# A gated linear recurrence and a two-layer MLP on one core: the order of all steps is found anew

## The chip, the cores and the metric

The kernel runs on one core of a Trainium2 chip. The metric is the device time of one execution in microseconds (us), as the median of several runs. Times of single instructions, positions and waits come from one profiled execution of the kernel.

Engines: PE is TensorE (matmul; PEld its weight loads), DVE is VectorE, ACT is ScalarE, POOL is GpSimd, SP is SyncE, which here issues every DMA.

## The reference

For each of 4 batches and 8 heads a complex-valued state is carried over 768 tokens; its result, 3072 tokens by 384, goes through an MLP with a leaky activation.

```python
mag = np.sqrt(a_re * a_re + a_im * a_im)
scale = np.minimum(mag, 0.999) / (mag + 1e-06)
a_re_n, a_im_n = (a_re * scale, a_im * scale)
for t in range(S):
    new_re = ar * S_re - ai * S_im
    new_im = ar * S_im + ai * S_re
    kv = np.einsum('bhd,bhe->bhde', k[:, :, t], v[:, :, t])
    S_re, S_im = (new_re + kv, new_im)
    y[:, :, t] = np.einsum('bhd,bhde->bhe', q[:, :, t], S_re)
x = attn_out.transpose(0, 2, 1, 3).reshape(B * S, H * D)
h = x @ w_in
g = np.maximum(h, 0.0) + alpha * np.minimum(h, 0.0)
return (g @ w_out).astype(np.float32)
```

Head dimension 48, `w_in` 384 x 2048, `w_out` 2048 x 384, all in float32 (the weights arrive as 64-bit words and are turned into float32 on the chip).

## The kernel before

The work is written as 41 generators, called tasks. Each `yield` ends a step; a step issues one instruction, or a few, on one engine (a PE step holds a burst of matmuls). Nothing is scheduled by a framework: a string, `ORDER` (lines 30 to 74), names one task per letter, and the plan advances that task by one step. So the string sets the order in which every engine and SP's queue are handed their instructions. Each engine works through what it is handed in that order, and waits where an input or a buffer is not ready.

```python
def run(self, order):
    for c in order:
        next(self.tasks[self.LETTERS.index(c)], None)
...
with tc.manual_schedule():
    for i, g in enumerate(GATES):
        plan.add(gates(i, *g))
...
    for u in range(NU):
        plan.add(unit(u))
    plan.add(loads_x())
    plan.add(all_mlp())
    plan.run(ORDER)
```

The tasks and their letters:

- `A` to `I`, `gates` (from line 224): the normalized gates and their running products, for batch 0 in three parts (1, 2 and 3 chunks of 128 tokens: A, B, C), then two parts of 3 chunks for each further batch. L251 loads the gates; L254 to L282 are ACT steps, L260 to L302 DVE steps; L319, L339 and L341 are the many products of the tree (on DVE for batch 0, the small ones on POOL for the others); L324 stores the decays, L427 and L430 make the phases, L422 and L432 store them. Two buffers `gate` are shared by all parts.
- `J`, `loads`: q and k of a unit (`KQ`, L580, L582), its phases (`PP`, L591, one buffer) and its decays (`T`, L598, two buffers). `K`, `half_rows`: copies of v in another row order (L561). `L`, `loads_v`: v (`V`, L607 to L612; `VL`, L630, L633).
- `M`, `pieces`: 16 pieces of the raw weights (L492, 768 KB each). `N` and `O`, `weights`: their conversion, with three ACT steps (L508, L510, L512), one POOL step (L516) and two DVE steps (L518, L520) for each.
- `P` to `Z` and `a` to `m`, `unit`: the 24 units, one chunk of 128 tokens of one batch each. DVE turns q and k by the phases (L665, L667) and runs the levels of a tree of decays (L721), PE makes the products within a level (L682), ACT copies operands and results (L744, L760, L703), DVE masks (L706). PE then transposes k (L789, copied by ACT in L791 and L792), makes the new state (L801; DVE L830, L833) and sums the output (L821, L845). ACT copies it (L859) into the unit's T, from where L864 stores it. T is free for the unit after the next one only then.
- `n`, `loads_x`: the stored outputs as the MLP's input (L877). `o`, `all_mlp`: for 14 groups of one or two units and 16 feature blocks each, PE's three matmuls (L893), ACT's negative part (L900), DVE's sum (L902), PE's output matmul (L912), ACT's copy (L922) and the store (L925). L893 writes one of two PSUM buffers; L902 frees it, so feature block k+2 waits for L902 of block k.

The first MLP work needs unit 0 complete and stored, and the first weights converted. The last needs unit 23.

## Time and profile before

| | us |
|---|---|
| median of 3 runs | 854.92 |
| the runs | 854.92, 858.98, 851.49 |
| span of the profiled execution (first to last instruction) | 851.8 |
| busy PE / DVE / ACT / POOL | 697.3 / 653.9 / 439.5 / 206.6 |

The page gives no other time of the profiled execution than its span, which lies 3.1 below the median and 0.3 above the fastest run. Busy time is the time in which an engine had at least one instruction under way; a share of the span hides stages with different limits, so the times by stretch of the span are read beside it. A group's row names the line, engine and operation, what it writes and reads, the shape and count, then total busy time, the mean of one in ns, and the idle time of the engine just before. A row of waits names the instruction that waited, what ended the wait, the total, the number of times and the longest.

### The profile page before, as it was taken

Reading aid. Unit: us, or ns where it says so; the run is one execution under the profiler, and the core shown is the slowest. Engines: PE = TensorE matmul, PEld = TensorE weight load, DVE = VectorE, ACT = ScalarE, POOL = GpSimd, SP = SyncE. Lnnn points to the kernel's source line nnn. Section 1 sums busy time; section 2 is a strip of 40 time slices with the busy share of each in tenths; the row PEclk is TensorE's granted clock in tenths of the full one; section 3 lists DMA queues with packets and bytes.
Section 4 is the critical chain, followed back from the end, with each engine's and each line's share of the span. In section 5 each row is a group of like instructions: output and inputs, shape, how many; then the busy total and the mean of one; then the engine's idle time right before and its main releaser. Section 6 shows DMA issues by size and latency. Waiting matters only on the chain.

```text
span 851.8 us, 26881 instructions
## 1 busy us (share of the span) xinstructions
PE 697.3 (82%) x11488; PEld 530.0 (62%) x11488; DVE 653.9 (77%) x1020; ACT 439.5 (52%) x937; POOL 206.6 (24%) x293
## 2 busy tenths in 40 slices
PE   0001414776998899899999999999999999999998
PEld 0001313565776677677777777777777777777776
DVE  5999999997997899599989986987776756633212
ACT  6767758766346754575476436554444334322221
POOL 6131232466403810270046044000052000000000
PEclk9999656798999999999999999999999999999999
DMA  8697977856779576877875887687554486412010
GB/s 238 140 286 173 245 187 232 221 133 134 179 192 197 120 164 171 185 159 168 240 152 130 219 157 183 146 189 177 130 119 99 142 157 124 89 44 65 11 39 9
DMA packets 194559, 130.92 MB, mean 154 GB/s; under 512 B 74504, under 2 KB 186248, under 8 KB 194440
## 3 DMA queue, kind: packets, MB, share of 16 engines
q1 hardware_dynamic: 194440, 129.20, 64.0%
q8 instruction: 90, 1.47, 0.8%
q14 instruction: 29, 0.24, 0.1%
HBM read 100.82 MB, written 35.71 MB: 160 GB/s over the span
## 4 chain that ended last, share of the span: by engine, by line
PE 58%; DVE 25%; DMA 7%; issue 3%; ACT 3%; SPq 3%; POOL 1%; DVEq 0%; ACTq 0%; POOLq 0%
PE ps_o L912 23%; PE ps_h L893 22%; DVE KQ L721 5%; PE ps_lv L682 4%; DVE gate L339 4%; DMA T<-decs 3%; PE ps_y L821 3%; DVE gate L427 2%; DVE gate L341 2%; PE ps_y L845 2%; PE ps_kv L801 2%; SPq L630 1%; DVE g_sb L902 1%; PE ps_kt L789 1%; DVE gate L430 1%
## 5 line engine op out<-in xcount | busy, mean ns | idle before, releaser
L912 PE MATMUL ps_o<-w_out_sb,g_sb 128*128 128x384 f32 x768 | 295.8, 498 | 12.8 <-DVE g_sb L902 10.0
L893 PE MATMUL ps_h<-xT,w_in_sb 128*128 128x256 f32 (+1 forms) x1344 | 299.5, 355 | 0.0
L893 PEld LDWEIGHTS ps_h<-xT,w_in_sb 128*128 128x128 f32 x1344 | 233.7, 192 | 71.1 <-issue 1.8
L902 DVE SCALAR_TENSOR_TENSOR g_sb<-g_sb,al,ps_h 128x256 f32<-128x256 f32 (+1 forms) x224 | 97.3, 436 | 131.6 <-ACT g_sb L900 131.2
L900 ACT ACTIVATE g_sb<-ps_h 128x256 f32<-128x256 f32 (+1 forms) x224 | 79.0, 354 | 201.5 <-PE ps_h L893 200.7
L912 PEld LDWEIGHTS ps_o<-w_out_sb,g_sb 128*128 128x128 f32 x768 | 137.1, 191 | 63.6 <-DVE g_sb L902 12.9
L721 DVE TENSOR_TENSOR KQ<-KQ,T 96x1024 f32<-96x1024 f32 x120 | 147.3, 1231 | 31.5 <-PE ps_lv L682 25.1
L682 PE MATMUL ps_lv<-WQ 96*32 96x32 f32 x2304 | 34.7, 204 | 79.3 <-DVE WQ L665 51.9
L682 PEld LDWEIGHTS ps_lv<-WQ 96*32 96x32 f32 x2304 | 26.8, 116 | 97.0 <-DVE WQ L665 51.9
L339 POOL TENSOR_TENSOR gate<-gate 128x72 f32<-128x72 f32 x42 | 23.9, 569 | 147.6 <-ACT gate L369 144.7
L744 ACT COPY WQ<-KQ 96x1024 f32<-96x1024 f32 x48 | 50.0, 1042 | 14.9 <-DVE KQ L721 14.8
L516 POOL TENSOR_SCALAR top<-top 128x768 f32<-128x768 f32 x16 | 39.2, 2454 | 70.1 <-ACT top L508 70.1
L760 ACT COPY W<-KQ 96x512 f32<-96x512 f32 x48 | 30.8, 642 | 43.7 <-DVE KQ L721 37.3
L339 DVE TENSOR_TENSOR gate<-gate 128x576 f32<-128x576 f32 (+5 forms) x84 | 49.9, 594 | 1.7
L859 ACT COPY T<-ps_y 48x256 f32<-48x256 f32 x96 | 30.8, 366 | 38.9 <-PE ps_y L845 38.3
L821 PE MATMUL ps_y<-A,VL 64*48 64x64 f32 x2304 | 43.3, 229 | 7.0 <-issue 5.6
L821 PEld LDWEIGHTS ps_y<-A,VL 64*48 64x48 f32 x2304 | 41.3, 129 | 7.9 <-issue 6.4
L789 PE MATMUL ps_kt<-ident,KQ 96*128 96x96 f32 x192 | 26.4, 263 | 22.3 <-DVE KQ L721 12.2
L427 DVE TENSOR_TENSOR gate<-gate 128x1152 f32<-128x1152 f32 (+2 forms) x36 | 44.2, 1250 | 0.1
L703 ACT ACTIVATE A<-ps_lv,columns 128x64 f32<-128x64 f32 x144 | 37.3, 336 | 13.0 <-PE ps_lv L682 12.8
L789 PEld LDWEIGHTS ps_kt<-ident,KQ 96*128 96x128 f32 x192 | 22.3, 150 | 30.9 <-ACT T L792 10.9
L801 PEld LDWEIGHTS ps_kv<-V,T 64*64 64x64 f32 x1408 | 28.0, 148 | 15.4 <-ACT T L792 8.7
(106 smaller groups left out, 927.2 us busy)
## 6 DMA issues: line engine op xcount, KB each, us to landing
T<-decs SPq DMA_DIRECT2D x48, 384.0 KB
PP<-phs SPq DMA_DIRECT2D x48, 193.5 KB
KQ<-in_q_dram SPq DMA_DIRECT2D x48, 192.0 KB
decs<-gate SPq DMA_DIRECT2D x7, 1152.0 KB
phs<-gate SPq DMA_DIRECT2D x14, 576.0 KB
KQ<-in_k_dram SPq DMA_DIRECT2D x40, 192.0 KB
vsc<-in_v_dram SPq DMA_DIRECT2D x48, 144.0 KB
VL<-vsc SPq DMA_DIRECT2D x24, 288.0 KB
```

The source lines that it names most:

```text
L339: on(4 * k).tensor_tensor(out=m, in0=w[:, 1::-1].unsqueeze(2).to_broadcast([P, 2, 2, k]), in1=pairs_of(u), op=ALU.mult)
L427: TT(out=m[:, a], in0=U5[:, 1 + a], in1=turned(off3, o)[:, a].unsqueeze(1).unsqueeze(3).to_broadcast([P, L // 2, nb, 2]), op=ALU.mult)
L682: nc.tensor.matmul(t[64 * i + j:64 * i + j + HC // 2, p], lhsT=keys(n, g), rhs=queries(n, g), start=True, stop=True)
L721: nc.vector.tensor_tensor(out=x, in0=x if x0 is None else x0, in1=m, op=ALU.mult)
L744: nc.scalar.copy(z.rearrange("p i n t -> p i (n t)").rearrange("p i (m h) -> p m i h", h=h), bass.AP(tensor=KQ.tensor, offset=KQ.offset + ...
L789: nc.tensor.transpose(t[:, p], KQ[:, 1, 4 * i + p], ident[:D2, :D2])
L801: nc.tensor.matmul(kv[s][j:j + HC, n], lhsT=T[rows, n, j:j + HC], rhs=V[rows, n // 2, (n % 2) * D:(n % 2 + 1) * D], start=True, stop=True)
L821: nc.tensor.matmul(o, lhsT=Vp[h][64 * i:64 * i + 64, s, e_ * D:(e_ + 1) * D], rhs=a, start=False, stop=False)
L893: nc.tensor.matmul(p, lhsT=w_in_sb[:, f // 2, kk, f % 2 * P:(f % 2 + 1) * P], rhs=x_of[m][:, kk], start=(kk == 0), stop=(kk == NK - 1))
L900: nc.scalar.activation(gt, p, AF.Relu, scale=-1.0)
L902: nc.vector.scalar_tensor_tensor(out=gt, in0=gt, scalar=al_1[:, f:f + 1], in1=p, op0=ALU.mult, op1=ALU.add)
L912: nc.tensor.matmul(sums[0], lhsT=gt[:, c * P:(c + 1) * P], rhs=w_out_sb[:, f], start=(f == 0), stop=(f == NF - 1))
```

## The change

Only the string changes. The tasks, their steps, shapes, engines and buffers are the same; each task's own steps keep their order, and only the interleaving of tasks differs. The first lines and the last ones of both strings (44 lines each), and those with the first MLP steps:

```diff
 ORDER = (
-    "AAAAAAAAAAAAAAAAAAAAABAAAAJMJJMABBBMMBANJMMAOAAAAAAAAAAAAAAAAAALLLNBLAAAAAAAAAAALNAAAAAAAKKKKKKKLLLA"
-    "OALLAMNNAAAAAAOAAAAAAAAABLBNAAAAAAALAANBBNOOBNBBBLBMBBBJJOJNOBBBBBNBBJNNNBBNBBBBOBBBBBBBBBBBBBBBNOPB"
-    "POBPPPPCCCBOKBBBBBBBBBBBBBPPOBBPKBCBBBMPCBPKKBCBJKKOPOPBBBBBBOMBKPNPMBBKNJBCKBBBBPPMBKKNKKBBNBPBBBBP"
...
-    "CCCCQRMLLNDCJQCNRNRLLCQCCLLLRMCQCQDQRJJOCOCKQODCCCCRDNQQQQCCQQQQQQJODMQLNNDQODDODoQEKoooooooDOoRooND"
...
-    "oooooooooooooooooooooooooooooooooooooooooooooooooooooooooooooooooooooooooooooooooooooooooooooooooooo"
+    "AAAAAAAAAAMMMMMMAAAAAAANAAAJJAJJAAAAAAAAAAAAAAAAAANNNNBAAAAOAOOANKONNNAKANABAAAAAAAAAAOAANABAAAAANA"
+    "AAAAAAABBMOAAAMANAAKKKKKKKKKKKKKBOBMBAAABALAAAABABBBBBBBABOOOBCCOBBBBBBBJJJJBBOBOBBBBOBOOBCBBOBBBCCJ"
+    "BNNNBNBBCBBBBCCPBNBMMOBPBBBBBBCBBLBLLPLLLLLNNNNNBKMBBBPBOOOOMLPBMBNKBCBBBPPPNPKKKKBKKBKBKBKBPBPBPOBC"
...
+    "LQQQnQJJooQQDQQCCCJKCCCCCCQKCRCCCCOOOOCQLCKQCQQQCRCoCooooQCoRooCDoLDooKLLLDLCCCCCCooJooooooLRRRRRLCC"
...
+    "nooooooooooooooooooooooooooooooooooooooooooooooooooooooooooooooooooooooooooooooooooooooooooooooooooo"
     "oooooooooooooooo")
```

The weight pieces (M) and their conversion (N, O) stand earlier, between the steps of the first gate part; the loads of gate part B stand later; unit 0 (P) is spread over a longer stretch, unit 1 (Q) over a shorter one; the first MLP steps (o) stand earlier in the string. From there on to the end the same letters come in other places with the same overall course.

## The prediction

> **What bounds the kernel now.** I read the page's busy table and groups first, then the busy times by stretch, then the waits of VectorE (DVE) and TensorE (PE), then the chain that ended last and SyncE's queue (SP). The page:

> ```profile
> PE 697.3 (82%) x11488; PEld 530.0 (62%) x11488; DVE 653.9 (77%) x1020; ACT 439.5 (52%) x937; POOL 206.6 (24%) x293
> ...
> L912 PE MATMUL ps_o<-w_out_sb,g_sb 128*128 128x384 f32 x768 | 295.8, 498 | 12.8 <-DVE g_sb L902 10.0
> L893 PE MATMUL ps_h<-xT,w_in_sb 128*128 128x256 f32 (+1 forms) x1344 | 299.5, 355 | 0.0
> ```

> No engine is full over the whole span, so the stretches matter (columns: span from:to, its length, busy PE, PE weight loads, DVE, ACT, POOL, granted PE clock, DMA share, GB/s):

> ```profile
> 0.00:100.00 100.00, 14.03 (x460) 11.90 (x460) 87.44 (x191) 70.47 (x105) 29.61 (x41) 0.97 0.86 221
> 100.00:150.00 50.00, 13.49 (x385) 11.59 (x386) 49.14 (x85) 36.38 (x57) 15.02 (x7) 0.55 0.75 203
> 150.00:200.00 50.00, 38.37 (x690) 29.57 (x690) 47.14 (x71) 35.89 (x71) 30.43 (x33) 0.90 0.74 174
> 200.00:250.00 50.00, 43.70 (x870) 34.66 (x868) 43.31 (x66) 21.19 (x53) 15.99 (x16) 0.93 0.71 176
> 250.00:300.00 50.00, 44.62 (x882) 34.64 (x878) 42.48 (x59) 33.30 (x73) 27.14 (x35) 0.97 0.74 147
> 300.00:350.00 50.00, 46.18 (x848) 34.65 (x847) 43.06 (x63) 20.00 (x51) 7.72 (x23) 0.97 0.77 184
> 350.00:600.00 250.00, 249.18 (x4059) 186.47 (x4058) 216.03 (x290) 141.20 (x307) 64.53 (x105) 1.00 0.75 171
> 600.00:852.00 252.00, 247.77 (x3311) 186.54 (x3309) 125.33 (x202) 81.09 (x224) 16.15 (x35) 1.00 0.38 86
> ```

> There are three stages. To 200 us DVE is full and PE mostly idle. From 200 to 350 both are some 85 to 92% busy, held up by each other. From 350 PE has no idle left (4 us in 250, of which the waits show 0.9 in one stretch). So the end is fixed at about 350 us: the time is when PE becomes full, plus the PE work left. PE idles 150 us before that and almost nothing after. An order can gain only before 350, and can lose anywhere.

> The waits of DVE between 150 and 350 us, then those of PE from 350 on (total, times, longest):

> ```profile
> DVE g_sb L902 <- ACT g_sb L900: 6.9, 6, 2.6
> DVE KQ L721 <- DMA T<-decs: 6.0, 3, 2.5
> DVE KQ L721 <- PE ps_lv L682: 3.4, 1, 3.4
> DVE KQ L721 <- ACT WQ L744: 3.0, 2, 2.6
> DVE St L833 <- PE ps_kv L801: 2.8, 1, 2.8
> ```
> ```profile
> PE ps_y L845 <- DVE St L833: 0.5, 1, 0.5
> PE ps_y L821 <- issue: 0.4, 1, 0.4
> ```

> The chain that ended last has the loads of T (the decays of a unit) in the middle stage (start, length):

> ```profile
> 219.39 7.44 DMA T<-decs
> ...
> 255.98 7.68 DMA T<-decs
> ```

> **A way to count.** Each engine keeps the order it is handed. I give every instruction the time it adds to its engine's busy time in the trace (PE: the mean of its form after 400 us, at full clock) and sum these in either order. The sum ahead of an instruction is its position: DVE ends at 653, PE at 669. The lag is its time in the trace less its position. PE's lag is 160 at position 62, 172 at 126, 177.7 at 176, and then 179 to 180 to the end: 669 + 179.5 + some 3 for the last store is the span of 851.8. So the forecast is a forecast of PE's final lag.

> DVE's L902 of feature block k frees the PSUM buffer that PE's L893 of block k+2 needs. So PE's lag is at least (DVE position after L902 of k) - (PE position of L893 of k+2) + DVE's lag there. Before, this difference and DVE's lag are 138.9 and 31.2 at k=48 (PE lag 172.1), 137.0 and 38.1 at k=62 (177.7), 128.9 and 49.5 at k=88 (179.8): they leave 1.4 to 2.6 for ACT's L900 and PE's start. The bound is tight, and DVE's work ahead of the features, plus what DVE waits, is what PE's start is made of.

> **The change, part by part.** All 1009 DVE, 935 ACT, 265 POOL, 755 SP and 5888 PE steps of the planned tasks are the same with the same shapes; only their places differ.

> *Work ahead of the features.* The differences, before -> after, are: k=8 126.2 -> 130.0; k=24 137.3 -> 134.3; k=40 136.8 -> 134.2; k=48 138.9 -> 130.4; k=56 137.4 -> 130.7; k=62 137.0 -> 133.3; k=64 133.8 -> 132.1; k=72 134.3 -> 126.8; k=88 128.9 -> 125.2; k=112 121.0 -> 117.4. From k=16 on the new order puts 2 to 8 us less DVE work ahead of the same PE work. The largest is 140.3 (k=50) before and 136.2 (k=42) after, and the new one comes early, while DVE's lag is still small.

> *Start.* Six weight steps of DVE instead of two (L518 0.55, L520 0.96 us each) stand inside gate task A's chain, and on SP the weight pieces are issued from 2.9 us instead of 8.2, with B's gate loads (L251) behind the store L324 (issued at 14.9). The first piece (768 KB) then has 9 us until ACT's L508 wants it at 12.2; at the 238 GB/s of the page's first slice it takes 3.2. B's first ACT step moves from ACT position 8.3 to 17.4, so its load, issued at about 15.4, is in time. DVE's lag at the end of A stays 11.6. I cost the start at 0; without that cover it is 2 us.

> *Unit 0 goes back, unit 1 forward.* Unit 0's last L721 ends at DVE position 80.1 instead of 67.3, unit 1's at 108.2 instead of 115.7, and the first L902 at 118.0 instead of 133.6. On SP, unit 0's stores (L864, second at 101.3 before) are issued at about 111, and 21 issues stand between them and unit 2's T load, against 3 before; everything behind L864 waits with it. Before, the same kinds of issue took:

> ```profile
> 111.58 3.39 SPq L492 DMA_DIRECT2D g_sb<-in_w_out_dram  x1
> 115.07 0.41 SPq L492 DMA_DIRECT2D g_sb<-in_w_in_dram  x1
> ...
> 116.21 3.22 SPq L607 DMA_DIRECT2D V<-in_v_dram  x1
> 119.47 2.13 SPq L609 DMA_DIRECT2D V<-in_v_dram  x1
> ...
> 122.39 3.30 SPq L630 DMA_DIRECT2D VL<-in_v_dram  x4
> ```

> At the fast rows (0.4 to 0.8 each) they take some 12 us, with slow ones such as these 21. T is issued at 123 to 132 and lands 6.0 to 7.7 later, at 129 to 140. Unit 2's first L721 is due at DVE position 118.1 plus a lag of 13.5, at 131.6. The wait is 0 to 8; I take 3.5, and the features wait for the same queue (their x load is the issue before T).

> *Later T loads.* T has two buffers, so unit u's load follows unit u-2's stores. From L833 of u-2 to L721 of u took 15 to 18 us where DVE waited (units 5, 6). DVE's own work between them goes from 14.5 to 21.1 for unit 5, 12.3 to 17.2 for unit 6, 17.1 to 22.4 for unit 9: most of the 6.0 us of waits goes. Unit 4 goes the other way, from 25.3 to 13.7: up to 4 us late; with one issue left between its store and load, where there were four, I take 1. The gain from the others: 4.

> *Local loops.* Where DVE hands to PE or ACT and needs the answer, I took the work there less DVE's own work in between. Before, this is positive by 4.4 us at unit 9 (L833 to PE's L845, L682 and back to L721; DVE waited 3.4 there) and by up to 1.4 on ACT around DVE positions 240 to 246 and 318. In the new order the largest are 1.9 and 0.2. Gain 3 on DVE's lag near position 315. For POOL the loops have 0.6 us to spare or more: 0.

> *After 350 us.* Loops through DVE shorter than 25 us are at most 0.1 us before and -0.4 after beyond PE position 170: nothing added.

> **The sum.** PE's lag after = difference + DVE's lag at that DVE position + 2. With the lag of before: k=42 136.2 + 28 + 2 = 166; k=64 132.1 + 38 + 2 = 172; k=88 125.2 + 49 + 2 = 176. Without the 4 and 3 above and with the 3.5 and 1 added, DVE's lag is 2.5 lower at the last two: 169.5 and 173.5. The row at k=88 keeps waits of DVE for a full PE (L902), which need not come back; the row at k=64 may lack new ones. I take the middle, 172: 7.5 under 179.5. The span is 851.8 - 7.5 = 844.3. The median of the runs, 854.92, is 3.1 above the profiled span: **847.4, say 847**.

> [...] PE's first features come 16 us of DVE work earlier but then stand in a sparse stretch. In this trace the clock is 0.50 from 100 to 140 us, where PE is busy 1 to 2 us in 10, and 1.00 from 150 to 160. [...] By the trace's rows PE idles over 80% of that stretch, so this adds nothing.

> **The rivals.** (1) *PE fills at once.* If DVE's waits past position 243 vanish, the largest difference decides: 136.2 + 24 to 28 + 2 = 162 to 166, a gain of 13.5 to 17.5: 840. For it: no loop is left over 2 us. Against it: DVE's lag grew from 17 at position 175 to 39 at 315. (2) *SP's queue becomes the wait.* If unit 2's T lands at 140 (8 us), unit 4's comes 4 late and the order behind them shifts by 3 more, DVE's lag is 15 higher where I took 4.5: 847 + 10.5 = 858, slower than before. It decides once these waits pass 12 us together; its far end is one wait as long as SP's longest, 20.2 us (behind L925), on top of my 4.5: 867. For it: issues of 3 us under load, SP waits of 77 us behind L864 and 104 behind L925. Against it: the vsc copies (L561), 5.8 us for two in that stretch before, are moved out of it. (3) *It does not do what it says:* DVE's waits for PE and T stay as they were, the lag at k=88 decides with the new 3.5: 179.5, no change: 855.

> **How the numbers follow.** Forecast 0.43 (842 to 852), rival 1 0.20 (835 to 842), rival 2 0.30 (852 to 868), rival 3 0.07 (852 to 858). A measurement here tells about 1% from no change: 846.4 to 863.5. Faster: rival 1 and under half of the forecast's case, 0.39. Slower: half of rival 2, 0.15. Within 1%: 0.46. The range, 837 to 864, leaves out the low end of rival 1 (0.06) and the high end of rival 2 (0.14).

> **What would show it.** PE's idle before it is full should fall from 150 to about 142 us, and from 250 to 350 us from 9 to 4; DVE's waits for T between 150 and 350 us from 6 to 3 or less; the first L902 should start near 132 to 136 instead of 147. Wrong would be: a wait of more than 8 us at unit 2's L721; PE idle of several us after 350; or DVE's lag over 40 at position 300.

## The result and the profile after

| | before | changed |
|---|---|---|
| median of 4 runs, us | 855.44 | 886.55 |
| lowest to highest | 851.49 to 858.98 | 875.09 to 891.86 |
| span of the profiled execution | 851.8 | 873.4 |

The changed kernel is slower: ratio 1.0286, 95% interval 1.0238 to 1.0334. Two of its four runs were disturbed and are left out of the ratio and of the medians further below; the other two took 875.09 (the profiled one) and 883.24 us. The forecast was 847, in a range of 837 to 864.

The page of the changed kernel: the busy table, then groups (busy, mean ns | idle before, and what ended it):

```profile
PE 704.4 (81%) x11488; PEld 535.5 (61%) x11488; DVE 654.3 (75%) x1020; ACT 441.9 (51%) x937; POOL 188.9 (22%) x293
...
L893 PE MATMUL ps_h<-xT,w_in_sb 128*128 128x256 f32 (+1 forms) x1344 | 302.5, 357 | 1.5 <-issue 1.5
L912 PE MATMUL ps_o<-w_out_sb,g_sb 128*128 128x384 f32 x768 | 295.2, 500 | 3.3 <-DVE g_sb L902 2.8
```

Busy times by stretch, the same columns as before the change (span, length, PE, weight loads, DVE, ACT, POOL, PE clock, DMA share, GB/s):

```profile
0.00:100.00 100.00, 9.83 (x345) 8.47 (x345) 87.69 (x193) 75.06 (x107) 38.10 (x44) 1.00 0.83 218
100.00:150.00 50.00, 23.46 (x583) 18.22 (x576) 44.14 (x83) 30.60 (x53) 6.14 (x2) 0.64 0.73 193
150.00:200.00 50.00, 37.26 (x617) 28.84 (x618) 48.60 (x70) 35.23 (x70) 24.96 (x28) 0.78 0.84 208
200.00:250.00 50.00, 47.88 (x955) 37.79 (x953) 48.33 (x73) 28.24 (x68) 17.74 (x23) 1.00 0.72 177
250.00:300.00 50.00, 42.40 (x864) 32.85 (x863) 38.35 (x54) 28.14 (x62) 17.44 (x31) 0.93 0.68 135
300.00:350.00 50.00, 45.22 (x702) 33.86 (x702) 43.84 (x62) 24.38 (x51) 7.60 (x14) 0.97 0.81 197
350.00:600.00 250.00, 236.01 (x3956) 178.03 (x3951) 202.30 (x271) 128.21 (x286) 60.48 (x114) 0.98 0.67 152
600.00:874.00 274.00, 262.32 (x3490) 197.46 (x3488) 141.04 (x221) 92.05 (x243) 16.43 (x39) 1.00 0.42 93
```

To 250 us PE has done 118 us of work, 9 more than before. Then it turns: from 350 to 600 PE idles 14.0 us where it idled 0.8. Waits of PE from 375 us on (total, times, longest), and links of the chain that ended last that are "issue", time in which PE waited for nothing that the profile shows (start, length):

```profile
PE ps_lv L682 <- issue: 9.5, 6, 3.0
PE ps_y L821 <- issue: 6.7, 4, 2.3
PE ps_y L845 <- issue: 3.5, 3, 1.7
PE ps_h L893 <- issue: 1.5, 2, 1.0
PE ps_o L912 <- ACT top L922: 0.3, 1, 0.3
```
```profile
408.17 2.29 issue
496.83 2.96 issue
529.18 1.91 issue
533.27 1.74 issue
561.76 1.31 issue
```

The profile names no engine, no buffer and no transfer behind them. PE's lag (its time less its position, as in the prediction) tells the same: at position 60 it is 154.4 (before 160.2), at 176 174.3 (177.7), at 200 174.5 (177.7). Then before keeps its lag, 179.4 at 250 and 179.0 at 660, and the changed kernel loses it: 181.4 at 250, 192.6 at 350, 198.9 at 500, 200.6 at 660. A lead of 3.2 us at 200 and a loss of 26.1 against 1.3 after it give 21.6, the difference of the spans.

Here is one stall in the timeline of PE (start, length, line, instructions, idle before):

```profile
406.00 1.15 PE L801 MATMUL ps_kv<-V,T 64*64 64x48 f32 x64
406.96 0.29 PE L812 MATMUL ps_y<-ident,nothing 64*48 64x256 bf16 x4
407.07 1.10 PE L821 MATMUL ps_y<-A,VL 64*48 64x64 f32 x60
410.46 0.71 PE L821 MATMUL ps_y<-A,VL 64*48 64x64 f32 x35 [2.29 <-issue]
```

It breaks off in the middle of one burst of L821, between two matmuls of one step with the same tiles, and PE's records show no wait for a semaphore there. So a late input of this burst is unlikely. And the profile has a DMA queue that the prediction never looked at:

```profile
q8 instruction: 90, 1.47, 0.7%
```

90 packets of 16 KB. PE has some 23,220 instructions (a float32 matmul is two weight loads and two matmuls here: L821's 1152 stand as x2304 of each on the page), 256 for a packet (in e1 below, with 2304 instructions fewer, there are 81 packets; e8's 9472 matmuls and weight loads have 37): so I take these packets to be PE's own program, loaded in blocks while it runs. The packet times say that a load takes 0.9 to 1.5 us in this run. All the longer stalls after 375 us end 1.2 to 1.6 us after such a load has landed (the one above at 410.46, its load from 407.38 to 408.88). That gave the theory: PE runs out of instructions, because bursts of tiny matmuls use a block of 256 up faster than the next one comes. The rivals: (A) late inputs (V, VL, T or SP's queue) that the waits don't name; (B) VectorE or ScalarE late from their new places.

### The profile page after: what moved, and what is told of

It is laid out like the page before. It is cut to its first block, busy times and chain, and to the rows that moved or that the text cites. A ratio compares the mean times of both kernels' runs of the same rounds, so it can differ in the third digit from the quotient of the medians.

```text
span 873.4 us, 26891 instructions
## 1 busy us (share of the span) xinstructions
PE 704.4 (81%) x11488; PEld 535.5 (61%) x11488; DVE 654.3 (75%) x1020; ACT 441.9 (51%) x937; POOL 188.9 (22%) x293
## 3 DMA queue, kind: packets, MB, share of 16 engines
q8 instruction: 90, 1.47, 0.7%
## 4 chain that ended last, share of the span: by engine, by line
PE 74%; DVE 15%; issue 6%; ACT 3%; POOL 1%; DMA 0%; DVEq 0%; ACTq 0%
PE ps_h L893 28%; PE ps_o L912 28%; PE ps_lv L682 5%; PE ps_y L821 4%; PE ps_y L845 3%; PE ps_kv L801 3%; DVE KQ L721 2%; PE ps_kt L789 2%; DVE gate L427 2%; DVE gate L339 2%; DVE gate L341 1%; DVE gate L430 1%; DVE top L518 1%; DVE gate L299 1%; DVE gate L319 1%
## 5 line engine op out<-in xcount | busy, mean ns | idle before, releaser
L893 PE MATMUL ps_h<-xT,w_in_sb 128*128 128x256 f32 (+1 forms) x1344 | 302.5, 357 | 1.5 <-issue 1.5
L912 PE MATMUL ps_o<-w_out_sb,g_sb 128*128 128x384 f32 x768 | 295.2, 500 | 3.3 <-DVE g_sb L902 2.8
L893 PEld LDWEIGHTS ps_h<-xT,w_in_sb 128*128 128x128 f32 x1344 | 234.5, 193 | 73.2 <-issue 3.9
L902 DVE SCALAR_TENSOR_TENSOR g_sb<-g_sb,al,ps_h 128x256 f32<-128x256 f32 (+1 forms) x224 | 97.3, 437 | 138.7 <-ACT g_sb L900 138.3
L900 ACT ACTIVATE g_sb<-ps_h 128x256 f32<-128x256 f32 (+1 forms) x224 | 78.6, 352 | 213.0 <-PE ps_h L893 211.5
L721 DVE TENSOR_TENSOR KQ<-KQ,T 96x1024 f32<-96x1024 f32 x120 | 148.0, 1234 | 47.3 <-PE ps_lv L682 32.3
L912 PEld LDWEIGHTS ps_o<-w_out_sb,g_sb 128*128 128x128 f32 x768 | 139.6, 193 | 56.0 <-DVE g_sb L902 4.5
L682 PE MATMUL ps_lv<-WQ 96*32 96x32 f32 x2304 | 35.3, 204 | 81.8 <-DVE WQ L665 54.7
L682 PEld LDWEIGHTS ps_lv<-WQ 96*32 96x32 f32 x2304 | 26.9, 116 | 102.5 <-DVE WQ L665 54.7
L744 ACT COPY WQ<-KQ 96x1024 f32<-96x1024 f32 x48 | 50.0, 1042 | 34.9 <-DVE KQ L721 34.2
L821 PE MATMUL ps_y<-A,VL 64*48 64x64 f32 x2304 | 44.9, 228 | 23.1 <-issue 23.1
L821 PEld LDWEIGHTS ps_y<-A,VL 64*48 64x48 f32 x2304 | 41.9, 128 | 24.8 <-issue 24.8
L516 POOL TENSOR_SCALAR top<-top 128x768 f32<-128x768 f32 x16 | 41.3, 2586 | 65.3 <-ACT top L508 65.3
L682 PE MATMUL ps_lv<-KQ,W 96*32 96x32 f32 x1536 | 25.6, 205 | 33.9 <-ACT W L760 25.6
L339 POOL TENSOR_TENSOR gate<-gate 128x72 f32<-128x72 f32 x42 | 21.3, 508 | 110.3 <-ACT gate L369 107.5
L427 DVE TENSOR_TENSOR gate<-gate 128x1152 f32<-128x1152 f32 (+2 forms) x36 | 42.4, 1216 | 0.6 <-POOL gate L412 0.4
L682 PEld LDWEIGHTS ps_lv<-KQ,W 96*32 96x32 f32 x1536 | 20.6, 114 | 34.3 <-ACT W L760 26.7
L706 DVE TENSOR_TENSOR A<-ps_lv,mask 128x256 f32<-128x256 f32 x96 | 37.2, 412 | 0.0
```

What stands on the lines that cost most here:

```text
L339: on(4 * k).tensor_tensor(out=m, in0=w[:, 1::-1].unsqueeze(2).to_broadcast([P, 2, 2, k]), in1=pairs_of(u), op=ALU.mult)
L427: TT(out=m[:, a], in0=U5[:, 1 + a], in1=turned(off3, o)[:, a].unsqueeze(1).unsqueeze(3).to_broadcast([P, L // 2, nb, 2]), op=ALU.mult)
L516: nc.gpsimd.tensor_scalar(out=top, in0=top, scalar1=F64_SMALL, scalar2=None, op0=ALU.max)
L682: nc.tensor.matmul(t[64 * i + j:64 * i + j + HC // 2, p], lhsT=keys(n, g), rhs=queries(n, g), start=True, stop=True)
L706: nc.vector.tensor_tensor(out=a.rearrange("p n (g t) -> p n g t", g=2), in0=t.unsqueeze(2).to_broadcast(whole), in1=masks[name].rearrange( ...
L721: nc.vector.tensor_tensor(out=x, in0=x if x0 is None else x0, in1=m, op=ALU.mult)
```

## Experiments

Terms. A *border* is a place in PE's program where a new block begins: by the stalls, where the number of PE's instructions in the trace (waits and branches among them) ahead of the first matmul behind the stall is 193 or 194 above a multiple of 256. *Past position 200* is the full stretch from some 375 us on. A block's *work* is its PE time by positions. The table counts, past position 200, what PE lost over 0.25 us between one matmul and the next beyond its own time: at a border (within 12 instructions behind one, 1.0 to 1.8 us after a load landed), in matmuls of L893 and L912 that took half-clock times (granted clock 0.50), and elsewhere. Lags and losses are those of the one profiled execution of each kernel. Losses under 0.25 us are in no column (some 7 us in e4), and e1 and e11 have some 11 us less PE work past position 200, so there the columns don't add up to the lag.

| run | median, us | ratio to before (interval) | PE's lag at 200, at 660 | at borders, us (times) | half clock | elsewhere |
|---|---|---|---|---|---|---|
| before | 855.4 | | 177.7, 179.0 | 0.6 (1) | 0 | 1.2 |
| changed | 879.2 | 1.029 (1.024 to 1.033) | 174.5, 200.6 | 24.5 (16) | 2.8 | 0.3 |
| e1 changed, half instructions | 855.6 | 1.001 (0.997 to 1.004) | 168.1, 183.0 | 17.7 (9) | 4.7 | 3.7 |
| e2 changed, then before | 868.1 | 1.016 (1.012 to 1.020) | 185.9, 193.3 | 3.0 (2) | 1.4 | 4.1 |
| e3 before, then changed | 886.6 | 1.038 (1.034 to 1.042) | 180.4, 212.6 | 24.1 (16) | 5.8 | 1.0 |
| e4 changed, respaced | 896.5 | 1.051 (1.044 to 1.058) | 174.7, 220.1 | 18.1 (10) | 7.4 | 12.7 |
| e5 before, shifted 76 | 891.8 | 1.042 (1.033 to 1.050) | 187.3, 208.9 | 19.5 (10) | 2.2 | 0.3 |
| e6 before, shifted 256 | 855.7 | 0.999 (0.996 to 1.003) | 178.8, 182.1 | 2.1 (2) | 0.4 | 1.4 |
| e7 changed, aligned | 879.7 | 1.030 (1.022 to 1.038) | 177.0, 206.3 | 5.8 (5) | 2.0 | 19.6 |
| e9 changed, aligned, gaps kept | 878.8 | 1.027 (1.020 to 1.034) | 173.4, 200.5 | 7.7 (8) | 1.4 | 15.7 |
| e10 changed, aligned, wider | 888.8 | 1.040 (1.035 to 1.044) | 179.6, 212.4 | 2.6 (3) | 2.5 | 22.7 |
| e11 before, half instructions | 850.8 | 0.996 (0.992 to 0.999) | 176.6, 178.2 | 6.3 (5) | 2.0 | 4.3 |
| e12 before, aligned | 855.9 | 1.002 (0.999 to 1.005) | 171.3, 176.8 | 0.5 (1) | 0 | 3.0 |
| e13 before, shifted 40 | 880.4 | 1.031 (1.026 to 1.035) | 188.3, 206.9 | 11.7 (5) | 5.0 | 2.0 |
| e14 before, shifted 12 | 860.3 | 1.006 (1.003 to 1.009) | 179.7, 186.8 | 5.5 (3) | 1.0 | 1.1 |
| e15 before, early part aligned | 850.5 | 0.997 (0.994 to 1.001) | 171.5, 175.9 | 3.0 (3) | 0 | 2.4 |
| e16 changed, shifted 44 | 882.5 | 1.036 (1.030 to 1.042) | 170.8, 205.0 | 26.5 (13) | 7.6 | 3.1 |

### Early or late: e2 and e3

e2 takes the first 1890 letters of the new string, then all that is left in before's order; e3 the first 1916 of before, then the new order. The first line of the string that differs, for e2 (against the changed string) and e3 (against before's):

```diff
-    "FFFYFooZZLoFooFoFFoFoFoFoFoYFJoYYGLYLLLLLLLGLoYYoooooooYYGooooooYYYZGJYZYZLYYKYooLLYYLoooooYYoKoYYKK"
+    "FFFYFooZZLoFooFoFFoFoFoFoFoYFJoYYGLYLLLLLLLGLoYYoooooooYYGooooooYYYZGJYZYZLYYKYooLLYYLooooFFFFFZZZFF"
...
-    "YoooooGZooGGoGGYYoYYJJJYoKKYGooYFFoFKKYoYLYLYLFLLLLYYLLLLFGaGZoYZFYYYFZZLZGKooooZooooLLoZKooFFFFFooo"
+    "YoooooGZooGGoGGYKKKKoooooKoKKYYYYYYJYJYLLJLZZLFZYYYYYYooooYFYLFLoFoooJJZKZKoooaoooZoooZooooaoFFFFFFF"
```

> The first 1890 letters of the new order (up to PE position 200, about 375 us), then all steps that are left in the order of before. Supply theory: the 3.4 us that the new order is ahead there are kept and its later stalls are gone: 848-855, PE's lag at the end 175 to 178. Rival A (loads and stores left in a worse state by the early part, felt later): the loss comes all the same, over 868. Rival B (the new order's VectorE and ScalarE places after 375 us): also 848-855; this run tells only early from late.

> The mirror: the first 1916 letters of the order of before (PE position 200), then the rest in the new order. Supply theory: before's lag at the seam (177.7) and the new order's later loss of some 24 us: 876-884, with 15 or so stalls of PE after 375 us that end about 1.4 us after a block of instructions has landed. Rival A (the early part does it): 852-860.

e3 came out a little over its range (886.6 for 876 to 884), far from rival A's 852 to 860, with the stalls that were expected (16 at borders): the new late part costs 32 us of lag on top of before's early part. In e2 the late part of before costs nothing: from position 225 (193.6) to 660 (193.3) the lag stands still. But e2 took 868, outside its range and where rival A begins; the lag decides against rival A all the same, since the loss was there before position 225: 7.7 us went at the seam (two waits there, 3.7 us at L801 for ScalarE and 1.8 at a border), and 9 before position 176, where it runs the changed kernel's own order. There the first L902 stood at 140.0 us instead of 134.7: one load of PE's program began at 133.2 us instead of 129.5, and PE waited for it. So most of the loss is made late, by the new late order; and two kernels with the same early order can part there by one load that begins later. Why it began later in e2 is not shown.

### Fewer instructions: e1 and e11

```diff
-                            o = halves(Y[64 * e_:64 * e_ + D, i, s], h)[:, :, 1]
-                            a = A[h][64 * i:64 * i + 64, 2 * s + e_]
+                            o = Y[64 * e_:64 * e_ + D, i, s]
+                            a = A[h][64 * i:64 * i + 64, 2 * s + e_].bitcast(BF16)[:, 1::2]
+                            w = Vp[h][64 * i:64 * i + 64, s, e_ * D:(e_ + 1) * D].bitcast(BF16)[:, 1::2]
+                            nc.tensor.matmul(o, lhsT=w, rhs=a.unsqueeze(2).to_broadcast([64, HC, 2]),
...
```

> The changed kernel, its order untouched; only L821 is altered: each matmul reads its operands as 16-bit numbers and writes twice the columns (128 instead of 64), so it is issued as one weight load and one matmul instead of two and two. Its part of the sum over the levels is then wrong; the columns streamed are the same, and PE's instructions fall by 2304. Supply theory (PE's instructions come in blocks of 256, one per 3.6 us or more, and bursts of tiny matmuls use them up faster): PE's waits for 'issue' at L821 fall from 23.1 us over the run to under 6, those after 350 us from 22 to under 8, and the time from 875-883 to 855-863. Rival A (late inputs: V, VL, T or SP's queue, which the waits fail to name): no input comes earlier, so the waits stay within 3 us and the time at 872-886. Rival B (VectorE or ScalarE are late from their new order): the same, 872-886.

> The kernel before with the edit of the half-instructions run: L821's matmuls as 16-bit ones with twice the columns, half the instructions (its part of the sum is wrong). By the bursts measured alone a 16-bit one with 128 columns takes 15.4 ns of PE (23.7 us for 1536) and a float32 pass with 64 columns 15.7 (36.2 for 2304), so the edit takes 1152 x 15.7 = 18 us of PE work away, not only instructions. If that is what the changed kernel gained by it, this one gains it too: 836-846, and the changed order still costs 12 to 20 us beside it. If the gain was the stalls alone, this one stays at 850-856.

e1's time, 855.6, is in the theory's range, but not for the reason given. The stalls did not go: 17.7 us at 9 borders instead of 24.5 at 16. The rest came from the edit's smaller PE work, which I had put at nothing (e8 below measured it after e1 had run; some 11 us of it lie past position 200), and from the early part, 6.4 us ahead of the changed kernel at position 200. e11 is the control: the same edit brings the kernel before only some 4 us, in the range (850 to 856) that had been given for a gain by the stalls alone. But it also lost more at borders (6.3 us at 5 of them instead of 0.6 at 1), 2.0 us at half clock and 3.1 more elsewhere, and the smaller work went into that. How much of e1's gain was stalls and how much was work can't be told apart. This pair speaks for the theory, but it isn't what settles it.

### The supply measured alone: e8

```python
def f64(count):
    for r in range(count):
        nc.tensor.matmul(ta[64 * (r % 2):64 * (r % 2) + D, r // 2 % 2, 64 * (r // 4 % 8):64 * (r // 4 % 8) + 64],
                         lhsT=x[64 * (r // 2 % 2):64 * (r // 2 % 2) + 64, 0:D], rhs=x[64 * (r // 2 % 2):64 * (r // 2 % 2) + 64, 64:128],
                         start=True, stop=True)
```

> Nothing of the kernel's work: PE alone runs bursts of 512 small float32 matmuls (48 x 64 columns, the form of L821; 2048 instructions, 8 blocks), of 1024 16-bit ones with 128 columns (2048 instructions), and of wide ones (128 x 256 columns) between them; the output is a constant. The first burst of small ones has loads of 12 MB beside it, the last has no DMA but PE's own code. Block theory: the bursts run at 3.2 to 3.8 us for 256 instructions once the first block or two are used up, with a pause at each border, and 25 to 30 us in all; with loads beside it pauses are longer and vary more. Rival (PE is never short of instructions; the waits were for data): 2.0 to 2.6 us for 256 instructions, evenly, 16 to 21 us a burst.

The last burst in PE's timeline, with no DMA beside it but the code:

```profile
245.07 3.34 PE L961 MATMUL ta<-x 64*48 64x64 f32 x223
249.44 2.00 PE L961 MATMUL ta<-x 64*48 64x64 f32 x128 [1.03 <-issue]
252.90 2.00 PE L961 MATMUL ta<-x 64*48 64x64 f32 x128 [1.45 <-issue]
256.62 2.00 PE L961 MATMUL ta<-x 64*48 64x64 f32 x128 [1.73 <-issue]
260.08 2.00 PE L961 MATMUL ta<-x 64*48 64x64 f32 x128 [1.45 <-issue]
```

128 matmuls with their 128 weight loads are one block: 2.00 us of work, then a pause of 1.45 us or a little more. The profile shows no wait for data here. In the bursts of small matmuls the pauses fall on every 256th PE instruction without exception, 3.45 us apart at the least and 4.0 at the most, and the bursts took 27.6 and 26.0 us, not 16. The loads put beside the first burst had ended when it began to pause, so what they do to it was not measured. From one border the steps are: the load begins 1.1 us after PE has entered the block before it, takes 1.0, and PE goes on 1.4 after the landing. So in these bursts a block took 3.45 us or more, and PE, with 2.00 us of work in each, waited at its end. In the wide bursts between them it was otherwise: there a load began 4.2 us before PE entered the block before it, and no border shows a pause. Behind wide matmuls a short block passed freely in the changed kernel too: 2 of its 16 did (650.18 and 781.62 us), their loads begun 4.3 and 1.9 us ahead of that entry.

### The same order with other borders: e5, e6, e13, e14, e16

The kernel before, with 19 matmuls (e5), 64 (e6), 10 (e13) or 3 (e14) ahead of everything; the changed kernel with 11 (e16):

```diff
+        first = ps.tile([P, 2, 512], F32, tag="y", name="ps_y")
+        for _ in range(19):
+            nc.tensor.matmul(first[0:D, 0, 0:HC], lhsT=ident[0:HC, 0:D], rhs=ident[0:HC, 0:HC], start=True, stop=True)
         plan.run(ORDER)
```

> The kernel before, order and all steps untouched, with 19 small extra matmuls (76 PE instructions) ahead of everything, where PE is idle. They only shift which of PE's instructions stand at the borders of its blocks of 256. Block theory (PE needs at least 3.3 us from one border to the next, because the load of the next block begins only there): by the order and the durations of before, the blocks past PE position 200 that hold less than 3.3 us of PE work go from 3 to 10 of 54, what they lack together from 1.8 to 12.2 us (in the changed kernel: 16 blocks, 18.9 us, and 25 us were lost). So 12.2 / 18.9 x 25 = 16 us: 866-876, with stalls of PE at L821, L845 and L682 that lie 256 instructions or a multiple of it apart. Rivals (order of the loads, places on VectorE or ScalarE): the order is that of before, 852-859.

> The control: the same with 64 extra matmuls, 256 instructions, one whole block. The borders fall on the same instructions as before: 3 blocks under 3.3 us past position 200, lacking 2.0 us. Block theory: 852-860, as before. If extra matmuls at the start cost by themselves (a wait, the clock), this one shows it, with three times as many of them: over 866.

> The kernel before with 10 small extra matmuls (40 PE instructions) ahead of everything: a dose between none and 76. Past position 200, 5 blocks of 55 are under 3.3 us and lack 4.9 us (before 3 and 1.8; shifted by 76: 10 and 12.2); from position 60 on 10.6 us are lacking (before 1.8, by 76: 17.6). Block theory: between the two, 862-876; PE's lag past position 200 grows by 5 to 9 us. If a shift did harm in another way (any number that is not a multiple of 256, or extra work on PE at the start), the harm would be that of 76, 880-892.

> The kernel before with 3 small extra matmuls (12 PE instructions) ahead of everything. Past position 200 no block is under 3.3 us, the lack to 5 us falls from 11.3 to 5.8; from 60 on to 16.2 from 18.7. Block theory: at least as fast as before, 850-856: the order of before sits within some 12 instructions of its best place. If any shift harms: over 860.

> The changed kernel with 11 small extra matmuls (44 PE instructions) ahead of everything, the best place of all for its order: past position 200 still 12 blocks of 55 are under 3.3 us and lack 17.2 us (unshifted 16 and 18.9). Block theory: its stretches of small matmuls are too long for any place of the borders, so 866-880, still far over before. If it is only bad luck in the place of the borders, as for the order of before shifted by 76: 850-858.

e5 and e6 settle that the place of the borders costs time. 76 more PE instructions in a stretch where PE idles, with the order of before untouched, cost 36 us; 256 of them cost nothing. Both rivals had said that e5 stays at 852 to 859. The same step of unit 20 in both timelines, e5 first:

```profile
709.15 0.29 PE L812 MATMUL ps_y<-ident,nothing 64*48 64x256 bf16 x4
709.26 1.50 PE L821 MATMUL ps_y<-A,VL 64*48 64x64 f32 x91
716.31 0.46 PE L821 MATMUL ps_y<-A,VL 64*48 64x64 f32 x5 [5.55 <-issue]
716.70 2.07 PE L893 MATMUL ps_h<-xT,w_in_sb 128*128 128x256 f32 x4
```
```profile
689.24 0.29 PE L812 MATMUL ps_y<-ident,nothing 64*48 64x256 bf16 x4
689.35 1.52 PE L821 MATMUL ps_y<-A,VL 64*48 64x64 f32 x96
690.80 1.13 PE L893 MATMUL ps_h<-xT,w_in_sb 128*128 128x256 f32 x4
```

In e6 the 96 matmuls run through in 1.52 us; in e5 a border stands after the 91st, and PE waits 5.55 us there. In the changed kernel, e3, e5, e13 and e16 every border stall over 0.5 us past position 200 stands at 193 or 194 in the count of 256, as every pause of e8 does. There, 3 of before's 54 blocks hold less than 3.3 us of work (1 to 4 by where in these few instructions the border is put), e5's 10 of 55, the changed kernel's 16 of 54. With the borders at other places the count gives the order of before 0 to 13 such blocks: it lies well where it is.

The sizes were off. e5 and e13 lost more than expected (892 for 866 to 876, 880 for 862 to 876), and e14, with no short block past position 200, still took 6 us more than before, outside its 850 to 856. By the time alone e13 and e14 came where their rival had put them, a harm by any shift (880 to 892, and over 860). But that harm would be the same for any shift, and the ratios were 1.006 for 12 instructions, 1.031 for 40, 1.042 for 76 and 0.999 for 256. And the traces show where it went: 11.7 us of e13's 18.6 past position 200 stand at five borders, 5.5 of e14's 7.1 at three, the longest of these between two matmuls of L893:

```profile
468.42 0.38 PE L893 MATMUL ps_h<-xT,w_in_sb 128*128 128x256 f32 x1
471.28 1.35 PE L893 MATMUL ps_h<-xT,w_in_sb 128*128 128x256 f32 x5 [2.49 <-issue]
```

My count took 3.3 us for every block. But in the changed kernel the loads ahead of three of the longest stalls (idle 3.0, 3.5 and 4.8 us, at 499.79, 314.45 and 259.90) began 2.6, 4.3 and 5.8 us after PE had entered the block before, not 1.1. So longer blocks were too short too: e14's three stalls stand behind blocks of 4.0, 4.0 and 4.4 us of work, the changed kernel's stall of 1.9 us at 531.09 behind one of 6.5. What delays a load is not shown here. e16 came near its range (882 for 866 to 880): 13 stalls at what the count gave as the best place for the new order. By the count the new order has 12 to 17 short blocks wherever the borders lie; other places than these two were not run.

### Filling the blocks: e4, e7, e9, e10

All four move PE's steps of the units and the MLP past each other in the new string (a line of e9's as a sample). e4 spread the work without regard to the borders; e7 and e9 changed PE's order only, by blocks; e10 gave VectorE and ScalarE 3 us of freedom too.

```diff
-    "ooSSTEDDooooToooTLLLLoDDTDooooooEUDJDDJTToTTonTTJTJJoTooooooooUTooDDDDDoTDooJooDDoooDDDoDTTTooTTTToT"
+    "oooSSTEDDooTooTLooLLLDDoTDEooUoDoJooDoDJTTTTonTTJooTJJoTooooUTDoDooDoDoDTDoJoDDooooDoDDDToToTToToTTT"
```

> The changed kernel with steps of units and of the MLP moved past each other from PE position 170 on, by at most 3.1 us of PE work, 4 us of VectorE or ScalarE work, so that 256 instructions in a row hold more PE work: summed over all such stretches, what is missing to 2.6 us falls from 7.9 to 3.2 us (before: 2.5), to 3.2 us from 16.3 to 7.8 (before: 6.7). Loads and stores keep their order on SP. Supply theory: the stalls of 22 us after 350 us fall to some 3 to 9, the time to 855-865. Rival A (late inputs): unchanged, 872-886. Rival B (VectorE's and ScalarE's places): moves by no more than a few us, 870-886.

> The changed kernel with PE's order alone altered: from PE position 60 on, steps of the MLP and of the units pass each other on PE by at most 2.7 us of PE work, chosen so that nearly every block of 256 instructions holds 3.3 us of PE work or more. VectorE, ScalarE, POOL and SP are handed exactly the changed kernel's order. Blocks under 3.3 us past position 200: from 16 to 2, lack from 18.9 to 1.6 us. Block theory: the 25 us lost after 375 us are gone but for 2 to 4: 848-858. Rivals (late inputs, VectorE's or ScalarE's places): unchanged, 872-886.

> As the run before it with PE's order alone altered (VectorE, ScalarE, POOL and SP keep the changed kernel's order; steps move by at most 2.7 us of PE work), but a unit's PE step that needs ScalarE or VectorE between keeps at least 1.3 us of other PE work ahead of it, where it had that: the earlier alignment took this work away and PE then waited 8.1 us at L801 and 2.5 at L789 for ScalarE. Past position 200, 4 blocks of 54 are under 3.3 us and lack 2.7 us (changed kernel: 16, 18.9). Block theory: stalls after 375 us under 8 us, waits for ScalarE under 4, 852-863. Rival (the places of the loads, of VectorE or of ScalarE hold it back): 872-886, with waits for them in the stalls' place.

> The same with more freedom: PE steps move by up to 4.7 us, VectorE's and ScalarE's by up to 3 us; 2 blocks of 54 under 3.3 us, lacking 0.6 us. Block theory: 846-858; if the changed kernel's lead at 375 us (3.4 us) is kept and nothing is lost after it, 849, below before. Rival: 872-886.

The time that the theory gave missed all four, and e7 and e9 came where the rivals had put them (872 to 886). But the stalls went as the theory said wherever the borders were counted: from 24.5 us to 5.8, 7.7 and 2.6. Waits that the changed kernel had not shown took their place. e7's from 375 us on:

```profile
PE ps_kv L801 <- ACT T L792: 8.1, 10, 1.2
PE ps_kt L789 <- ACT T L792: 2.5, 4, 0.7
PE ps_o L912 <- ACT top L922: 2.0, 4, 1.0
PE ps_y L845 <- issue: 2.0, 2, 1.2
PE ps_lv L682 <- issue: 2.0, 2, 1.3
```

The work that fills a block was taken from between L789 and L801, where it had covered ScalarE's copies. e9 kept 1.3 us there and still waited 4.6 at L801; e10 waited 7.8 at L682 for ScalarE's W instead. e4 kept 10 border stalls, put wide matmuls right behind them, where they ran at half clock (7.4 us), and lost 12.7 us elsewhere. So the rivals hold this much: the orders that fill the blocks are held by ScalarE instead. What the changed order itself would take without its stalls, and whether some order near it has neither loss, stays open.

### Filling the blocks of the kernel before: e12 and e15

The same filling in the kernel before, on PE alone (e12), and only between positions 60 and 195 (e15). The first line that differs in e15:

```diff
-    "LoLoDKUooooooLDDTDJJooooJJnKDDDoEEooooDooTTETooDooooooLUoooooooooEoTToooUUDDLoooooooDTooToooooooDLDU"
+    "LoLoDKUooooooLDDTDJJooJooJnoKoDDDoEooEooDTTEoToooooDooLoooUooEoToooTooUooUoDDoLooooDoooTToooDoLooDUo"
```

> The kernel before, PE's order alone altered by at most 2.3 us of PE work so that the blocks hold more: from position 60 on, those under 3.3 us go from 4 to 1 of 75, the lack to 5 us from 18.7 to 7.8. Block theory: PE's stalls at 290.9, 338.7 and 344.7 us (6.4 us together) shrink, of which some is hidden by VectorE's pace: 848-854. Rival (an order found with all waits in view can't be touched without new ones): 856-864.

> The kernel before with PE's order altered only between positions 60 and 195 (by at most 2.3 us of PE work), where the aligned version of before gained 6 us of PE's lag, which it gave back later in its altered part; from there on the order and the borders are those of before. Block theory: the gain stays, 846-852, ahead of both kernels. If the early gain is only the one profiled execution's, 853-857.

In e15 PE's lag is 171.5 at position 200 (before 177.7) and 175.9 at the end (before 179.0), so half of the early lead was lost again; 3.0 us of stalls stand at borders there. The median is 850.5, in its range, but the interval of the ratio, 0.994 to 1.001, does not clear it from no change. e12 gained as much early and gave it back late (171.3 to 176.8); its 855.9 lies outside its range.

## Why the prediction was wrong

1. *The way to count, and the early part: right in the main.* The first L902 stands at 134.7 us (forecast 132 to 136, before 147.4). DVE's waits for T between 150 and 350 us fell from 6.0 to 1.6 (forecast 3 or less), and no L721 waited 8 us, so rival 2 did not come. PE's idle to 350 us fell from 150 to 144 (forecast 142). PE's lag was to be 172, and was 174.3 at position 176; at position 200 the lead over before was 3.2 us of the 7.5 forecast. From 250 to 350 us PE idled 12.4 us where 4 was forecast. PE's waits in that stretch:

```profile
PE ps_y L821 <- issue: 11.0, 4, 4.8
PE ps_y L845 <- issue: 1.4, 1, 1.4
```

All of it is stalls of the kind above, and VectorE waited behind them (L902 for L900, 11.8 us from 150 to 350): its lag at position 300 is 38.7 instead of 32.0.

2. *The step that failed: "After 350 us. Loops through DVE shorter than 25 us are at most 0.1 us before and -0.4 after beyond PE position 170: nothing added."* Past position 200 PE lost 24.8 us more than in before. The step priced every wait of PE for another engine and found none; there were none (0.3 us for ScalarE). It took the order of PE's own instructions to be free, because PE's work is the same sum in any order. The runs show that PE has one more input, its program, in bursts of small matmuls 256 instructions per 3.45 us at best (e8), and that the new order has 16 blocks that hold less than 3.3 us, where before has 3; 24.5 us stand at 16 borders in its trace.

3. *There was a sign beforehand.* Before had "PE ps_y L821 <- issue: 0.4" after 350 us and larger waits of this kind from 150 to 375 us, and its page has the row of the instruction queue (q8 instruction: 90, 1.47, 0.8%). The largest of these waits:

```profile
PE ps_o L912 <- issue: 2.5, 1, 2.5
PE ps_y L821 <- issue: 2.0, 1, 2.0
```

The prediction showed the row after 350 us and did not ask what it was, though it named "PE idle of several us after 350" as the sign of being wrong.

4. *The sparse start.* PE's clock was 0.64 from 100 to 150 us and 0.78 to 200 (before 0.55 and 0.90), and PE's lag at position 60 was still 5.8 lower than before. So adding nothing for the sparse start did no harm to the forecast; what the clock cost there was not measured.

## What to carry over

The order of tiny matmuls was here also an order of program blocks: count PE's instructions (a float32 matmul was four), cut them every 256, and see that each piece holds the 3.45 us of PE work that a block took at best in e8, better more (stalls stood behind pieces of 4.0 to 6.5 us in e14 and the changed kernel). Filling the pieces wasn't free: in e7, e9 and e10 other waits took the stalls' place (8.1 and 4.6 us at L801, 7.8 at L682). Where PE stalls on "issue" in the middle of a burst, shift the borders by some matmuls at the start and see whether the stalls move, as in e5 and e6 (19.5 us at 10 borders with 76 instructions, 2.1 at 2 with 256): then the program's supply is the likely cause. The order of before, which lies well for its borders, lost some per cent by a small edit ahead of it (3 matmuls: 0.6%, 10: 3.1%, 19: 4.2%).

## What the runs showed of the hardware that I had not expected

```profile
402.00:408.00 6.00, 6.00 (x147) 4.67 (x146) 6.00 (x10) 3.96 (x7) 0.00 (x0) 1.00 1.09 280
408.00:410.00 2.00, 0.17 (x11) 0.02 (x1) 1.86 (x4) 0.05 (x1) 0.00 (x0) 1.00 0.96 168
410.00:412.00 2.00, 1.54 (x100) 1.46 (x99) 0.18 (x1) 0.00 (x0) 0.00 (x0) 0.83 0.05 13
412.00:417.00 5.00, 4.81 (x49) 3.59 (x41) 2.82 (x3) 1.76 (x5) 0.12 (x1) 0.50 0.11 24
417.00:422.00 5.00, 5.00 (x18) 3.44 (x17) 3.11 (x4) 2.25 (x4) 0.00 (x0) 0.89 0.81 223
```

  The wide matmuls that fell into this stretch took up to twice their time: from 412.0 to 416.5 us two of L912 took 925 ns and two of L893 631 in the mean, against 487 and 398 from 417.5 to 440. In e4 this came to some 7.4 us in all, in e16 to 7.6.
- 16-bit matmuls with 128 columns took as long as float32 passes with 64 (15.4 and 15.7 ns each in the bursts), so half the instructions was also half the work.
